# A fallback path written as a loop of 16 turns, its scratch laid out by block, and twelve first loads moved from ScalarE's DMA queue to SyncE's

## The chip, the cores and the metric

The kernel runs on one core of one Trainium2 chip. The metric is the device time of one execution in microseconds (us). Three runs of the kernel before gave 1262.43, 1261.22 and 1262.65 us, so the median is 1262.43 us.

## What is computed

One input `x` of 2048 rows and 512 columns goes through two branches, which are mixed row by row by a gate:

```python
def _A_ref(x, wq, wk, wv, wo):          # H = 32 query heads of 16, one shared key and value head
    q = (x @ wq).reshape(B, S, H, Dh).transpose(0, 2, 1, 3)
    k = x @ wk
    v = x @ wv
    scores = einsum("bhqd,bkd->bhqk", q, k) * (Dh ** -0.5)
    p = softmax(scores, axis=-1)
    o = einsum("bhqk,bkd->bhqd", p, v)
    return o.transpose(0, 2, 1, 3).reshape(B, S, H * Dh) @ wo
def _B_ref(x, w_gate, w_up, w_down):
    return (gelu(x @ w_gate) * (x @ w_up)) @ w_down
g = sigmoid((x * gate_w).sum(-1, keepdims=True))
out = g * a + (1 - g) * b
```

The weights `wq` and `wk` are drawn eight times larger than the others.

## The kernel before

**Prologue (the first 72 us).** `x` arrives transposed, in four groups of 512 rows. For each group TensorE projects K and V together (`pk`) and then four blocks of 128 columns of Q (`pq`, eight heads each). Every operand is split into a high part and a low part, and three products are summed. ScalarE and VectorE split each block of Q into `q2`, and `post_q` (L198) stores it to the scratch `scr` in DRAM with one DMA on SyncE's queue (SP), L213. The groups run in the order 1, 2, 3, 0, so that the last blocks stored are those of group 0, which attention reads first.

**Loads of Q.** Attention walks 64 half-blocks `u` of four heads (two buffers `Q`, one per `u` in turn). `load_q(u)` fills a buffer with six DMAs: four from `scr` (L275, L276) and two from the scratch `shs` (L285), which holds three extra rows per head that shift the exponent. In the general case these rows hold minus the row maximum; else they are zero, zero and one, written once by four DMAs on GpSimd's queue (L171). The loads of `u` = 0 and `u` = 1 are issued on ScalarE's queue (ACT), after the Q blocks 2 and 3 of the last group; all later ones on SP.

**The choice of path.** `pairmax` (L310) bounds the largest score from the largest absolute Q and K, sets `flag`, and fills one row, `zz[0:1]`, of 2048 values with a shift (L318), which two DMAs on ACT copy into rows 50 and 114 of the key tile `kp` (L320). All five engines then load `flag` into a register (L518) and branch (`tc.If`, L519). With these inputs the flag is 0 and the general path is skipped. The general path computes all scores once more to take the row maxima: written out, it is 2,048 matmuls, 1,024 reductions and 128 loads, and its code lies between the branch and what follows.

**DMA counters.** Each DMA on SP or ACT counts on one of eight semaphores (`DMAHW0` to `DMAHW7`), dealt in turn when the program is built. A DMA whose semaphore is still owed by an earlier one waits on its issuing engine until the earlier one has landed. On the path that is not taken, SP waits for all eight and then adds to each what the skipped path would have added (eight semaphore instructions at L519). What comes after the branch and reads loaded data waits for the counts after that addition.

**Main part.** 1024 score tiles: two matmuls (L576), one exponential on ScalarE (L579), four products with V (L649). Between them the matmuls of the second branch (L358) are dealt by the words of the table `WORDS`, two at a time on the two halves of the array. This order is fixed by hand and is the same before and after.

Of the kernel before, what the change touches and what calls it, by code (L numbers as in the profile page):

```python
# [9 lines left out]
F32 = mybir.dt.float32  # L10
# [9 lines left out]
P = 128  # L20
S = 2048
D = 512
H = 32
# [36 lines left out]
def mix_kernel(ctx, tc, xT, wq, wkv, wo, wf, out):  # L60
# [137 lines left out]
    def post_q(tg, b, pq, last):  # L198
        q2 = p2.tile([P, 2, TG], F32R, tag="q2", name=f"q2{tg}_{b}", bufs=3)
        i = tg * NB + b  # L200

        def bound():
            nc.vector.tensor_reduce(qmx[:, i : i + 1], pq, axis=AX, op=ALU.max, apply_absolute_value=True)
# [5 lines left out]
        nc.scalar.copy(q2[:, 0], pq)  # L209
        if not last:  # L210
            bound()
        nc.vector.tensor_sub(q2[:, 1], pq, q2[:, 0])
        nc.sync.dma_start(scr[tg, b].rearrange("(t d) h q -> (d h) t q", t=2), q2.bitcast(F32))  # L213

    chunks = [(tg, f) for tg in range(NTG) for f in range(NF)]
    W = {}
# [50 lines left out]

    Q = {}

    def load_qk(t, u, q):  # L270
        g, ub = divmod(u, 8)
        b, a = divmod(ub, 2)
        for j in range(2):
            hs = slice(4 * a + j, 4 * a + 4, 2)
            q.dma_start(t[64 * j : 64 * j + 32].bitcast(F32), scr[g, b, 0:32, hs])  # L275
            q.dma_start(t[64 * j + 32 : 64 * j + KR].bitcast(F32), scr[g, b, 0:16, hs])  # L276

    def load_q(u, shift=True, data=True, q=nc.sync):
        g, ub = divmod(u, 8)
        if data:  # L280
            Q[u] = cp.tile([P, 2, TG], F32R, tag="Q", name=f"Q{u}", bufs=2)
            load_qk(Q[u], u, q)
        if shift:
            for j in range(2):
                q.dma_start(Q[u][64 * j + KR : 64 * j + QK].bitcast(F32), shs[g, :, 4 * ub + j : 4 * ub + 4 : 2])  # L285

    fetch_w(0)
    fetch_w(1)
    for ti, tg in enumerate(order):
        xh, xl = xs[tg]  # L290
        pk = ps_a.tile([P, TG], F32, tag="pa", name=f"pk{tg}")
        passes(pk, lambda c: wkh[:, c], lambda c: wkl[:, c], lambda c: xh[:, c], lambda c: xl[:, c], NC)
        post_k(tg, pk)
        for b in range(NB):
            pq = two_banks(f"pq{tg}_{b}")[:, 0:TG]
            bs = slice(b * P, (b + 1) * P)
            passes(pq, lambda c: wqh[:, c, bs], lambda c: wql[:, c, bs], lambda c: xh[:, c], lambda c: xl[:, c], NC)
            if ti + 1 < NTG:
                split_x(order[ti + 1], b)
            post_q(tg, b, pq, ti == NTG - 1 and b == NB - 1)  # L300
            if ti == NTG - 1 and b == 0:
                for part in split_w(0):
                    part()
            if ti == NTG - 1 and b == 1:
                post_v()
            if ti == NTG - 1 and b >= 2:
                load_q(b - 2, q=nc.scalar)

    def pairmax():
# [6 lines left out]
        nc.vector.tensor_scalar(sh, cb, -1.01 * DH, None, op0=ALU.mult)  # L316
        row = zz[0:1].rearrange("p a b -> p (a b)")
        nc.vector.tensor_scalar(row, row, 0.0, sh[0:1], op0=ALU.mult, op1=ALU.add)  # L318
        for r in (QK - 1, 64 + QK - 1):
            nc.scalar.dma_start(kp[r : r + 1].bitcast(F32), row.bitcast(F32))  # L320

    acc = {}
    O = {}
# [195 lines left out]
    with tc.If(v > 0):  # L519
        with tc.tile_pool(name="gp", bufs=1) as gp:  # L520
            zr = gp.tile([1, S], F32, name="zr")
            nc.vector.memset(zr, 0.0)
            for r in (QK - 1, 64 + QK - 1):
                nc.sync.dma_start(kp[r : r + 1].bitcast(F32), zr)
            for g in range(NTG):
                mx = gp.tile([P, 4, H, 2], F32, tag="mx", name=f"mx{g}")
                for ub in range(8):
                    t = gp.tile([P, 2, TG], F32R, tag="gq", name=f"gq{g}_{ub}", bufs=2)
                    load_qk(t, 8 * g + ub, nc.sync)
                    for i in range(4):  # L530
                        for h in range(4):
                            rs = slice(64 * (h % 2), 64 * (h % 2) + KR)
                            for e in range(2):
                                ps = two_banks("gs")
                                for j in range(2):
                                    k0 = e * 1024 + j * 512
                                    nc.tensor.matmul(ps[:, j * 512 : (j + 1) * 512],
                                                     t[rs, h // 2, i * P : (i + 1) * P],
                                                     kp[rs, k0 : k0 + 512], start=True, stop=True)
                                nc.vector.tensor_reduce(mx[:, i, 4 * ub + h, e : e + 1], ps, axis=AX, op=ALU.max)  # L540
                m1 = gp.tile([P, 4, H], F32, tag="m1", name=f"m1{g}")
                nc.vector.tensor_reduce(m1, mx, axis=AX, op=ALU.max)
                pt = ps_f.tile([P, TG], F32, tag="pf", name=f"pt{g}")
                for i in range(4):
                    nc.tensor.transpose(pt[0:H, i * P : (i + 1) * P], m1[:, i], ident)
                nm = gp.tile([H, TG], F32, tag="nm", name=f"nm{g}")
                nb = gp.tile([H, 3, TG], F32R, tag="nb", name=f"nb{g}")
                nc.vector.tensor_scalar(nm, pt[0:H], -1.0, None, op0=ALU.mult)
                nc.vector.memset(nb[:, 2].bitcast(F32), 1.0)
                nc.vector.tensor_copy(nb[:, 0], nm)  # L550
                nc.vector.tensor_sub(nb[:, 1], nm, nb[:, 0])
                nc.sync.dma_start(shs[g].rearrange("r h q -> h r q"), nb.bitcast(F32))
# [217 lines left out]
```

## Time and profile before

| | |
|---|---|
| median of three runs | 1262.43 us (1261.22 to 1262.65) |
| span of the profiled execution | 1262.1 us |
| matmuls executed | 9,884 |
| TensorE / ScalarE / VectorE / GpSimd busy | 99% / 82% / 45% / 18% |
| instruction fetches, queues q8 and q14 | 80 packets and 35 packets |

No time of the profiled execution is listed beside its span of 1262.1 us; it lies 0.3 us under the median of the runs and inside their spread. In the views, PE is TensorE's matmuls and PEld its weight loads, DVE VectorE, ACT ScalarE, POOL GpSimd, SP SyncE; a name with a q behind it (SPq, PEq) is the engine's sequencer, that is an instruction that issues a DMA, branches, or handles a semaphore or register. Times in the views are counted from the first instruction.

### The profile page before, as it was taken

The numbers are of one execution on the slowest core, as the hardware profiler recorded it, in microseconds if no ns is written. First come the engines' busy times: TensorE is split into PE (matmuls) and PEld (weight loads), VectorE is DVE, ScalarE is ACT, GpSimd is POOL, SyncE is SP. The second block draws the span as 40 slices with busy tenths as digits, with TensorE's granted clock in tenths as the row PEclk, the third lists the DMA queues.
The fourth block names the chain that finished last, engine by engine and source line by source line (L and its number), as shares of the span: only waits on it lengthen the run. The fifth ranks groups of instructions, "written<-read, shape, count | busy, mean of one in ns | idle before, by whom it ended". The sixth has DMA issues, their size and how long they took to land.

```text
span 1262.1 us, 23901 instructions
## 1 busy us (share of the span) xinstructions
PE 1248.1 (99%) x9884; PEld 669.8 (53%) x9884; DVE 572.8 (45%) x860; ACT 1031.1 (82%) x1118; POOL 221.7 (18%) x261
## 2 busy tenths in 40 slices
PE   9989999999999999999999999999999999999998
PEld 6855555555455555545555555554544555455454
DVE  6762352635453163453546146362546324445334
ACT  5358888888898888888888888888887888888893
POOL 3132211201320020211131012120232002112100
PEclk9989999999999999999999999999999999999999
DMA  8441111111210111211030021011111013011000
GB/s 316 163 159 56 40 42 49 39 39 56 81 39 14 63 61 39 64 39 56 23 97 2 31 81 64 16 63 39 47 53 63 15 31 106 22 43 39 15 1 34
DMA packets 26371, 72.67 MB, mean 58 GB/s; under 512 B 4016, under 2 KB 4048, under 8 KB 26256
## 3 DMA queue, kind: packets, MB, share of 16 engines
q1 hardware_dynamic: 25244, 69.17, 16.5%
q8 instruction: 80, 1.31, 0.4%
q10 hardware_dynamic: 756, 1.11, 0.3%
q0 software_dynamic: 256, 0.79, 0.2%
q14 instruction: 35, 0.29, 0.1%
HBM read 57.67 MB, written 13.37 MB: 56 GB/s over the span
## 4 chain that ended last, share of the span: by engine, by line
PE 92%; ACT 1%; DVE 1%; issue 0%; POOL 0%; ACTq 0%
PE acc L649 37%; PE s L576 23%; PE z L358 18%; PE y L358 13%; ACT p L579 1%; PE wos L343 1%; DVE acc L466 0%; PE wof L343 0%; DVE sq L386 0%; POOL mark L366 0%; DVE sq L387 0%; DVE gs L394 0%; DVE n L600 0%; DVE gs L383 0%; ACT sq L390 0%
## 5 line engine op out<-in xcount | busy, mean ns | idle before, releaser
L579 ACT ACTIVATE p<-s 128x1024 f32<-128x1024 f32 x1024 | 979.8, 1025 | 176.2 <-PE s L576 169.0
L649 PE MATMUL acc<-p,v 128*32 128x512 f32 x4096 | 490.8, 598 | 0.0
L576 PE MATMUL s<-Q,kp 51*128 51x512 f32 x2048 | 392.2, 420 | 5.9 <-SPq L519 3.2
L576 PEld LDWEIGHTS s<-Q,kp 51*128 51x128 f32 x2048 | 188.1, 185 | 247.9 <-ACT p L579 167.5
L649 PEld LDWEIGHTS acc<-p,v 128*32 128x32 f32 x4096 | 107.7, 109 | 246.7 <-issue 241.1
L128 POOL TENSOR_TENSOR gl<-st,gh 128x512 fp32r<-128x512 f32 x88 | 123.9, 1429 | 400.1 <-PE s L576 177.4
L383 DVE COPY gs<-z 128x512 f32<-128x512 f32 x43 | 29.8, 692 | 247.6 <-PE z L358 124.6
L358 PE MATMUL y<-xh,gh 64*128 64x512 f32 x344 | 138.9, 404 | 1.5 <-DVE gs L394 1.5
L358 PE MATMUL z<-xh,gh 64*128 64x512 f32 x344 | 139.0, 404 | 0.7 <-POOL mark L366 0.7
L358 PE MATMUL z<-xl,gh 64*128 64x512 f32 x344 | 135.7, 394 | 0.0
L358 PE MATMUL y<-xl,gh 64*128 64x512 f32 x344 | 135.5, 394 | 0.0
L358 PE MATMUL y<-xh,gl 64*128 64x512 f32 x344 | 135.2, 393 | 0.0
L358 PE MATMUL z<-xh,gl 64*128 64x512 f32 x344 | 135.1, 393 | 0.0
L366 POOL MEMSET mark<- 1x1 f32 x81 | 8.5, 104 | 585.6 <-PE y L358 583.6
L456 DVE SCALAR_TENSOR_TENSOR acc<-z,gc,acc 128x512 f32<-128x512 f32 x24 | 18.0, 751 | 146.5 <-PE z L358 106.0
L358 PEld LDWEIGHTS z<-xh,gh 64*128 64x128 f32 x344 | 64.6, 188 | 16.0 <-POOL mark L366 8.8
L358 PEld LDWEIGHTS z<-xh,gl 64*128 64x128 f32 x344 | 64.3, 187 | 8.9
L358 PE MATMUL z<-dh,hh 64*128 64x512 f32 x176 | 69.0, 392 | 0.0
L358 PE MATMUL z<-dh,hl 64*128 64x512 f32 x176 | 68.9, 392 | 0.0
L358 PE MATMUL y<-dh,hh 64*128 64x512 f32 x176 | 68.9, 391 | 0.0
L358 PE MATMUL y<-dh,hl 64*128 64x512 f32 x176 | 68.8, 391 | 0.0
L358 PEld LDWEIGHTS z<-xl,gh 64*128 64x128 f32 x344 | 64.8, 188 | 7.6
(147 smaller groups left out, 1583.4 us busy)
## 6 DMA issues: line engine op xcount, KB each, us to landing
st<-wf SPq DMA_DIRECT2D x44, 768.0 KB
scr<-q SPq DMA_DIRECT2D x16, 512.0 KB
Q<-scr SPq DMA_DIRECT2D x60, 128.0 KB
out<-acc SPq DMA_DIRECT2D x16, 256.0 KB
Q<-scr SPq DMA_DIRECT2D x60, 64.0 KB
xr<-xT SPq DMA_DIRECT2D x6, 512.0 KB
xst<-xT SPq DMA_DIRECT2D x12, 256.0 KB
xr<-xT SPq DMA_DIRECT2D x4, 256.0 KB
```

The costliest lines, as they stand in the source:

```text
L128: eng_l.tensor_sub(lo, src, hi)
L343: nc.tensor.matmul(ps, a, b, start=(first and q == 0), stop=(last and q == len(terms) - 1), skip_group_check=True)
L358: mm = nc.tensor.matmul(ps, a[rs], b[rs], start=(half == 0 and q == 0), stop=(half == 1 and q == len(X) - 1), skip_group_check=True)
L366: relay = nc.gpsimd.memset(mark, 0.0).ins
L383: nc.vector.tensor_copy(gs, g)
L456: nc.vector.scalar_tensor_tensor(o, ps, w, o, op0=ALU.mult, op1=ALU.add)
L576: nc.tensor.matmul(ps[:, j * TG : (j + 1) * TG], kp[rs, kc * P : (kc + 1) * P], Q[u][rs, pr], start=True, stop=True)
L579: nc.scalar.activation(p, ps, AF.Exp, bias=0.0, scale=SCALE)
L649: nc.tensor.matmul(accp[u][32 * j : 32 * j + 32], vt[:, kc], pb[s, j // 2][:, (j % 2) * TG : (j % 2 + 1) * TG], start=(kc == 0), stop=(kc ...
```

## The change

Four edits go together. The general path becomes a loop over 16 blocks (`tc.For_i`), whose body handles two half-blocks. `scr` and `shs` are indexed by block, so that the loop can address them by a register; the initial fill of `shs` is four DMAs by head within a half-block in place of four by group of rows. The first twelve loads of Q go to SP's queue. The shift row has 512 values and is copied into `kp` four times over by a repeating source.

```diff
-    scr = dr.tile([NTG, NB, 32, 8, TG], F32, name="scr")
-    shs = dr.tile([NTG, 3, H, TG], F32, name="shs")
+    scr = dr.tile([NTG * NB, 32, 8, TG], F32, name="scr")
+    shs = dr.tile([NTG * NB, 2, 3, 4, TG], F32, name="shs")
...
-    for g in range(NTG):
-        nc.gpsimd.dma_start(shs[g].rearrange("r h q -> h r q"), zz[:, 0:3].bitcast(F32))
+    for h in range(4):
+        nc.gpsimd.dma_start(shs[:, :, :, h].rearrange("g a r q -> (g a) r q"), zz[:, 0:3].bitcast(F32))
...
-                load_q(b - 2, q=nc.scalar)
+                load_q(b - 2)
...
-        row = zz[0:1].rearrange("p a b -> p (a b)")
-        nc.vector.tensor_scalar(row, row, 0.0, sh[0:1], op0=ALU.mult, op1=ALU.add)
+        nc.vector.tensor_scalar(zz[0:1, 3], zz[0:1, 3], 0.0, sh[0:1], op0=ALU.mult, op1=ALU.add)
         for r in (QK - 1, 64 + QK - 1):
-            nc.scalar.dma_start(kp[r : r + 1].bitcast(F32), row.bitcast(F32))
+            nc.scalar.dma_start(kp[r : r + 1].bitcast(F32).rearrange("p (c q) -> p c q", c=4),
+                                zz[0:1, 3:4].bitcast(F32).broadcast_to([1, 4, TG]))
...
-            for g in range(NTG):
-                mx = gp.tile([P, 4, H, 2], F32, tag="mx", name=f"mx{g}")
-                for ub in range(8):
-                    t = gp.tile([P, 2, TG], F32R, tag="gq", name=f"gq{g}_{ub}", bufs=2)
-                    load_qk(t, 8 * g + ub, nc.sync)
+            with tc.For_i(0, NTG * NB, 1) as gb:
+                for a in range(2):
+                    t = gp.tile([P, 2, TG], F32R, tag="gq", name=f"gq{a}", bufs=2)
+                    load_qk(t, scr[bass.ds(gb, 1)].rearrange("o r h q -> (o r) h q"), a)
...
-            load_q(0, data=False)
-            load_q(1, data=False)
+            load_shift(0)
+            load_shift(1)
```

SP, from the store of the third Q block of group 0 to the branch (`scr<-q` is a store, `Q_587` and `Q_614` are the buffers of `u` = 0 and `u` = 1, and what a row waits for stands in brackets). Before:

```order
L213 DMA scr<-q_2_582 128x2x512 [waits DMAHW6_49,DVE_49,Activation_49]
L213 DMA scr<-q_3_607 128x2x512 [waits DMAHW5_49,DVE_49]
L518 TENSOR_LOAD flag [waits DVE_49]
L518 ISA x2
L519 COMPARE_AND_BRANCH
```

The same place on SP of the change, from the second load of `Q_587` to the last of `Q_614` (ahead of these rows stand the same store of the third block and the first load of `Q_587`, behind them the flag and the branch):

```order
L274 DMA Q_587<-scr 16x2x512 [waits DMAHW7_49]
L273 DMA Q_587<-scr 32x2x512 [waits DMAHW1_49]
L274 DMA Q_587<-scr 16x2x512 [waits DMAHW2_49]
L279 DMA Q_587<-shs 3x2x512 [waits DMAHW4_49,DMASW2_49,DMASW0_49]
L279 DMA Q_587<-shs 3x2x512 [waits DMAHW5_49,DMASW3_49,DMASW1_49]
L213 DMA scr<-q_3_607 128x2x512 [waits DMAHW6_49,DVE_49]
L273 DMA Q_614<-scr 32x2x512 [waits DMAHW7_49]
L274 DMA Q_614<-scr 16x2x512 [waits DMAHW0_49]
L273 DMA Q_614<-scr 32x2x512 [waits DMAHW1_49]
L274 DMA Q_614<-scr 16x2x512 [waits DMAHW2_49]
L279 DMA Q_614<-shs 3x2x512 [waits DMAHW3_49]
L279 DMA Q_614<-shs 3x2x512 [waits DMAHW4_49]
```

Twelve loads now stand ahead of SP's load of the flag, and the store of the last block stands behind six of them. The store of the third block now counts on semaphore 5 and the first load of `Q_587` on 6, so the last load of `Q_587` waits until that store has landed, and the store of the last block waits until that first load has. The semaphores 0 and 3, which the loads of `Q_587` skip in the turn, are those of the two copies into `kp` on ACT: the second load of `Q_614` waits for the first copy to land, and the fifth for the second copy.

ACT, from its last conversion of Q to the copies into `kp`. Before:

```order
L209 CAST q_3_607<-pq_3_594 128x512 [waits DVE_49,Activation_49]
L275 DMA Q_614<-scr 32x2x512 [waits DMAHW4_49]
L276 DMA Q_614<-scr 16x2x512 [waits DMAHW6_49]
L275 DMA Q_614<-scr 32x2x512 [waits DMAHW7_49]
L276 DMA Q_614<-scr 16x2x512 [waits DMAHW0_49]
L285 DMA Q_614<-shs 3x2x512 [waits DMAHW1_49]
L285 DMA Q_614<-shs 3x2x512 [waits DMAHW2_49]
L320 DMA kp<-woh 1x16x128 [waits DMAHW3_49,DVE_49]
L320 DMA kp<-woh 1x16x128 [waits DMAHW4_49]
```

And in the change:

```order
L209 CAST q_2_582<-pq_2_569 128x512 [waits DVE_49,DMAHW2_49,PE_49,Activation_49]
L209 CAST q_3_607<-pq_3_594 128x512 [waits DMAHW3_49,DVE_49,Activation_49]
L318 DMA kp<-woh 1x4x512 [waits DVE_49]
L318 DMA kp<-woh 1x4x512
L517 TENSOR_LOAD flag [waits DVE_49]
L518 COMPARE_AND_BRANCH
```

ACT's two copies into `kp` follow its last conversion directly and wait for VectorE alone.

TensorE, the whole of what lies between its branch and the first score matmul in the change (`gs` are the scores of the general path, `pt` its transposed maxima):

```order
L518 COMPARE_AND_BRANCH
L524 COMPARE_AND_BRANCH
L524 UNCONDITIONAL_BRANCH x2
L764 BRANCH_PREFETCH_HINT
L536 MATMUL gs<-kp,gq_708 128x512 x64
L544 MATMUL pt_844<-ident,m_842 4x128 x4
L536 MATMUL gs<-kp,gq_856 128x512 x64
L544 MATMUL pt_992<-ident,m_990 4x128 x4
L524 REGISTER_ALU
L524 COMPARE_AND_BRANCH
L524 UNCONDITIONAL_BRANCH
L518 UNCONDITIONAL_BRANCH x2
```

Before, 32 rows of 64 such matmuls and four of four transposes stood there: 2,064 matmuls, each with a weight load, against 136 now. On VectorE 1,024 reductions became 64, and on SP 128 loads became eight. Behind the branch the order on every engine is that of before.

More of the change, by code (lines that the diff above doesn't have):

```diff
@@ L212, in post_q @@
         nc.vector.tensor_sub(q2[:, 1], pq, q2[:, 0])
[L213 removed]
+        nc.sync.dma_start(scr[i].rearrange("(t d) h q -> (d h) t q", t=2), q2.bitcast(F32))
     chunks = [(tg, f) for tg in range(NTG) for f in range(NF)]
@@ L268, in mix_kernel, with load_qk, load_shift, load_q @@
     Q = {}
-    def load_qk(t, u, q):
-        g, ub = divmod(u, 8)
-        b, a = divmod(ub, 2)
+    def load_qk(t, rows, a):
         for j in range(2):
             hs = slice(4 * a + j, 4 * a + 4, 2)
[L275 to L285, printed above, removed]
+            nc.sync.dma_start(t[64 * j : 64 * j + 32].bitcast(F32), rows[0:32, hs])
+            nc.sync.dma_start(t[64 * j + 32 : 64 * j + KR].bitcast(F32), rows[0:16, hs])
+    def load_shift(u):
+        gb, a = divmod(u, 2)
+        for j in range(2):
+            nc.sync.dma_start(Q[u][64 * j + KR : 64 * j + QK].bitcast(F32), shs[gb, a, :, j::2])
+    def load_q(u):
+        Q[u] = cp.tile([P, 2, TG], F32R, tag="Q", name=f"Q{u}", bufs=2)
+        load_qk(Q[u], scr[u // 2], u % 2)
+        load_shift(u)
     fetch_w(0)
```

27 lines of the change are left out of this document (14 added, 13 removed).

## The prediction

> **What bounds the kernel now.** I read the page first, then the waits, then one place closely.
>
> ```profile
> span 1262.1 us, 23901 instructions
> PE 1248.1 (99%) x9884; PEld 669.8 (53%) x9884; DVE 572.8 (45%) x860; ACT 1031.1 (82%) x1118; POOL 221.7 (18%) x261
> PE 92%; ACT 1%; DVE 1%; issue 0%; POOL 0%; ACTq 0%
> q8 instruction: 80, 1.31, 0.4%
> ```
>
> TensorE is busy 99% of the span and holds 92% of the chain that ended last. So a microsecond that TensorE loses or wins anywhere moves the end by about as much. The change leaves TensorE's order alone, so I look for what TensorE waits for where the change acts, around the branch at 60 to 80 us. The waits name it:
>
> ```profile
> PEld s L576 <- PEq L519: 3.5, 1, 3.5
> PE s L576 <- SPq L519: 3.2, 1, 3.2
> DVE dh L127 <- DVEq L519: 1.9, 1, 1.9
> PE s L576 <- issue: 1.4, 1, 1.4
> ```
>
> ```profile
> 72.65 0.70 PE L576 MATMUL s<-Q,kp 51*128 51x512 f32 x2 [3.15 <-SPq L519]
> ```
>
> Before the first score matmul, at 72.65 (start, duration, and in brackets the idle time before it), TensorE's matmuls stand still for 3.15 us, that is from 69.5, released by SP's semaphores of the branch; shortly after they do so for another 1.4 us for which no waiting shows. A third loss is only seen in the clock. These are stretches of 3.41 us; the columns are the stretch, its length, then the busy time of PE, PEld, DVE, ACT and POOL (instructions), the granted clock, DMA share and GB/s.
>
> ```profile
> 63.66:67.07 3.41, 3.41 (x18) 2.72 (x16) 2.41 (x9) 0.59 (x1) 0.00 (x0) 1.00 1.00 319
> 67.07:70.49 3.42, 2.42 (x11) 1.69 (x9) 2.52 (x4) 0.00 (x0) 1.16 (x1) 1.00 0.70 224
> 70.49:73.90 3.41, 1.25 (x8) 1.07 (x9) 2.41 (x3) 0.46 (x1) 3.05 (x3) 1.00 0.26 41
> 73.90:77.31 3.41, 2.02 (x11) 1.82 (x10) 2.54 (x5) 2.18 (x3) 0.07 (x1) 0.50 0.86 252
> 77.31:80.73 3.42, 3.42 (x19) 3.37 (x16) 0.58 (x1) 1.63 (x3) 0.00 (x0) 0.50 0.46 188
> 80.73:84.14 3.41, 3.41 (x30) 2.63 (x28) 2.46 (x5) 3.26 (x5) 2.11 (x3) 1.00 0.00 0
> 954.54:957.95 3.41, 1.94 (x15) 1.28 (x17) 3.26 (x6) 1.79 (x3) 0.00 (x0) 1.00 0.00 0
> 957.95:961.36 3.41, 3.41 (x20) 2.66 (x18) 3.41 (x4) 1.77 (x3) 3.03 (x2) 0.50 0.00 0
> ```
>
> After a stretch in which PE was busy 1.25, 2.02 or 1.94 us the next one ran at half clock; after 2.42 us or more it ran at full clock. So the stall costs more than its length: 73.90 to 80.73 us holds 2.02 + 3.42 us of work at half speed, 2.72 us lost. TensorE loses here 3.2 + 1.4 + 2.7 = 7.3 us in all, and that is what the change can move.
>
> **The branch itself.** Columns of the next view: line, engine, operation, count, duration min/median/max in ns, first and last start in us.
>
> ```profile
> L519 SPq EVENT_SEMAPHORE  x8: 17/17/17, 71.7 to 72.5; - x8
> L519 DVEq COMPARE_BRANCH  x1: 72/72/72, 68.1 to 68.1; - x1
> L519 PEldq COMPARE_BRANCH  x1: 3892/3892/3892, 68.1 to 68.1; - x1
> L519 SPq COMPARE_BRANCH  x1: 45/45/45, 68.4 to 68.4; - x1
> L519 DVEq EVENT_SEMAPHORE  x1: 21/21/21, 71.3 to 71.3; - x1
> L519 ACTq COMPARE_BRANCH  x1: 54/54/54, 71.9 to 71.9; - x1
> ```
>
> TensorE's branch takes 3.9 us, to 72.0; VectorE's next instruction comes 3.2 us behind its branch; on ACT, where nothing is skipped, a branch takes 0.05 us. Packets of the instruction queues lie in the same stretch (69 to 71.4 us, first fence), and one more on q8 at 72.7 to 74.4 us, the place of the second stall (second fence):
>
> ```profile
> q8 instruction: 1, 0.02, 3.0%
> q14 instruction: 2, 0.02, 2.9%
> ```
>
> ```profile
> q8 instruction: 1, 0.02, 5.3%
> ```
>
> So I read the branch as a jump to code that is not there yet. On the page q8 brought 1.31 MB in 80 packets for 2 x 9,884 TensorE instructions, some 250 a packet. The jump was over 2,064 matmuls with weight loads, about 4,130 instructions or 16 packets; it becomes 136, about 270. I take it that the target is then there and that both q8 stalls go: **minus 1.4 us** for the second; the first only uncovers the other wait. The Trainium skill, page "Runtime: NRT & Kernel Launch", section "Instruction fetch mechanics", says that instructions are fetched in blocks of 256, the next block while one runs, and that a taken branch out of these two blocks waits for a fetch. The packets agree; by that rule 270 instructions are within reach only from the first part of a block, and about a hundred, as on SP and VectorE, from any. Out of reach, the 1.4 us could come back, and the sum below would be plus 0.4.
>
> **The other wait: SP's eight semaphores.** They end at 72.5, TensorE starts at 72.65. Before, what lands last ahead of them are the copies into `kp`, late because ACT issues the loads of `u` = 1 first:
>
> ```profile
> 64.64 0.59 ACT L209 CAST q<-pq 128x512 fp32r<-128x512 f32 x1 [2.95 <-DVE qmx L203]
> 64.66 0.31 ACTq L275 DMA_DIRECT2D Q<-scr  x1
> 67.13 0.31 ACTq L276 DMA_DIRECT2D Q<-scr  x1
> 69.21 1.81 ACTq L320 DMA_DIRECT2D kp<-woh  x2
> ```
>
> ```profile
> 63.07 3.27 SPq L213 DMA_DIRECT2D scr<-q  x2
> ```
>
> ```profile
> 66.82 0.13 DVE L316 TENSOR_SCALAR sh<-cb 1x1 f32<-1x1 f32 x1
> 67.05 1.27 DVE L318 TENSOR_SCALAR woh<-woh,sh 1x2048 fp32r<-1x2048 f32 x1
> ```
>
> The load at 67.13 stood until the store issued at 63.07 had landed, 4.06 us; the copies were issued by 71.02 and had landed within 1.5 us of that, by SP's last semaphore. In the change ACT is free. The row has 512 values: 0.13 + (1.27 - 0.13) / 4 = 0.42 us, so it is ready at 67.4, and the first copy goes out 1.8 us sooner than before. It lands between 69.0 (1.5 us later, the issue free) and 71.5 (4.06 later); I take 69.8, by the row of the copies themselves: 0.9 us of issue, half of 1.81, and 1.5.
>
> But SP now issues the loads, and the second load of `u` = 1 waits for that first copy. Behind it stand four more loads, SP's load of the flag, and the eight semaphores, for which TensorE waits. SP's price for loads and flag:
>
> ```profile
> 112.48 0.42 SPq L276 DMA_DIRECT2D Q<-scr  x1
> 114.54 0.36 SPq L227 DMA_DIRECT2D st<-wf  x1
> ```
>
> ```profile
> L518 SPq TENSOR_LOAD <-flag x1: 1060/1060/1060, 66.9 to 66.9; - x1
> ```
>
> The last five of six such loads take 114.54 - 112.48 = 2.06 us: done at 71.9. The flag's load started at 66.9 and the branch came at 68.4: 1.5 us, to 73.4. Eight semaphores, 71.7 to 72.5, are 0.8 us: 74.2. The last load, issued at about 71.6, lands by 73.4 at best and 75.7 at worst. The rest of the SP chain lies ahead of it: the store issued at 63.07 lands by 67.1, then the last store and the first load of `u` = 1 go out by 68, before the copy has landed; that costs nothing unless the copy lands before 68. So TensorE resumes at **74.2** instead of 72.65 (73.4 with the copy at 69.0, 77.6 in the first rival): plus 1.55 us. Behind SP's loads and flag stands the first weight fetch of the main part:
>
> ```profile
> 72.65 1.95 SPq L227 DMA_DIRECT2D st<-wf  x2
> ```
>
> ```profile
> 81.62 0.76 DVE L127 CAST gh<-st 128x512 fp32r<-128x512 f32 x2
> ```
>
> It has 9 us until VectorE splits its weights at 81.6, of which 1.55 go; no term, and if the cover were short, at most that much.
>
> **The clock after it.** With the stretches where they are, 70.49 to 73.90 is idle and 73.90 to 77.31 runs at half clock, with 3.1 us of work: full clock from 77.31, loss 1.55 us against 2.72, so **minus 1.2 us**. If the stretches fall elsewhere the loss is 1.1 to 2.8 us.
>
> **The rest at nothing.** The first six loads that leave ACT stood in the 2.95 us in which its conversion waited for VectorE, so that stays at 64.64. VectorE's 1.9 us and 0.85 us of the shorter row come free while TensorE stands still, so they are hidden; without that cover they would be worth 2.7 us at most. The fill of `shs` is four DMAs of 192 KB before and after, issued 50 us ahead of their readers.
>
> **Sum.** Before 3.15 + 1.4 + 2.7 = 7.25; after 4.7 (69.5 to 74.2) + 0 + 1.55 = 6.25. That is minus 1.0 us on a span of 1262.1; on the median of 1262.43, which is 0.3 above the span, **1261.4 us**. About 0.2%, or 2.5 us, is what a measurement of this kernel can tell from no change.
>
> **Rivals.**
> *The SP chain runs late (slower).* If each landing takes the 4.06 us of the store, the copy lands at 71.5, the loads end at 73.5, the last lands at 77.3 and TensorE resumes at 77.6: 8.1 idle and 1.6 of clock, 9.7 against 7.25, 1264.9 us. It decides at about 75.2: later than that, the stretch to 77.31 holds under 2.1 us of work and the half clock lasts to 80.73. For it: the stores and loads did take that long at 60 to 67 us. Against it: that was with the DMA engines 100% and 70% busy up to 70.49, and 26% after it. Chance 0.2.
> *The short code does not shorten the jump.* TensorE's 3.9 us stay hidden (72.0 is before 74.2), but SP's own branch comes at 73.4 and 3.3 us (68.4 to 71.7 before) go on top: resumed at 77.5, again 2.3 us worse, 1264.7. For it: no row shows a jump over a hundred instructions. Against it: ACT's 0.05 us. Chance 0.12.
> *SP's loads wait for nothing that matters.* Twelve loads at 0.41 from 63.45 end at 68.4; the last lands at 71.0, between 1.5 and 4.06 us behind, and the semaphores end at 71.2. TensorE is idle for 1.8 us, the stretch from 70.49 holds 2.6 us of work, and by the 2.42 row the clock stays: 1.8 against 7.25, so 1257.0. Chance 0.08, since the order shows the waits. The Trainium skill, page "DMA: Bandwidth & Descriptors", section "Issuing engines are not separate DMA queues", says that the issuing engine only decides who spends the issue time; by that alone this case would hold. In this trace the wait at 67.13 speaks against it.
>
> **How the numbers follow.** The forecast has 0.6: 1261.4, and 1259.6 to 1262.8 by itself, the stretches' 1.1 to 2.8 and the half-clock stretch at 957.95, which costs 1.7 us and may or may not return when everything shifts by 1 us. The range, 1258.8 to 1265.2, takes in both slower rivals' prices and leaves out the third rival. Faster than 1259.9: 0.08 from the third rival and 0.09 from the forecast, 0.17. Slower than 1264.95: half of 0.32, with a little less as both lie just under it, 0.14. Within: 0.69.
>
> **What would show it.** TensorE's branch under 0.2 us and no q8 packet right behind it; VectorE's wait at the branch gone. SP's first load of `u` = 1 by 68, the second near 69.8, its flag at 71.9, its semaphores ending near 74.2, and TensorE idle 69.5 to 74.2 with no second stall; half clock for one stretch. Copies into `kp` out at 67.4. Wrong would be: SP's semaphores 3 us behind its branch, a resumption before 73 or after 75.2, or a difference that arises behind 85 us.

## The result and the profile after

| | before | change |
|---|---|---|
| median | 1262.04 us (1261.13 to 1263.56, 6 runs) | 1266.22 us (1265.68 to 1266.86, 6 runs) |
| ratio | | 1.0034, 95% interval 1.0022 to 1.0045 |
| span of the profiled execution | 1262.1 us | 1265.1 us (its time: 1266.86 us) |

The change is 4.2 us slower; 1261.4 us was predicted. The page of the change first, as far as it answers to that of before:

```profile
span 1265.1 us, 23904 instructions
PE 1246.6 (99%) x9884; PEld 668.5 (53%) x9884; DVE 573.2 (45%) x860; ACT 1030.4 (81%) x1118; POOL 222.4 (18%) x261
q8 instruction: 79, 1.29, 0.4%
```

TensorE has the same work (1248.1 us before), so the loss is waiting. The waits show one of 7.6 us where before had 3.2 and 1.4, and the instructions of the branch show which engine came last:

```profile
PE s L574 <- SPq L518: 7.6, 1, 7.6
```

```profile
L518 SPq EVENT_SEMAPHORE  x8: 17/17/17, 76.2 to 76.7; - x8
L518 PEldq COMPARE_BRANCH  x1: 352/352/352, 67.4 to 67.4; - x1
L518 DVEq COMPARE_BRANCH  x1: 72/72/72, 67.7 to 67.7; - x1
...
L518 SPq COMPARE_BRANCH  x1: 45/45/45, 75.6 to 75.6; - x1
```

TensorE's branch takes 0.35 us instead of 3.9, and SP's semaphores follow its branch by 0.6 us instead of 3.3: the short code does what it was expected to do. (Not all of the 3.3 us is the jump: a load of `u` = 1 landed at 71.68 in before, just ahead of the first semaphore. Experiments 3 and 15 have 2.5 and 2.7 us with nothing left to land.) But SP branches at 75.6 instead of 68.4. The timeline of the change shows why (start, duration; SP's rows, and between them the copies on ACT and TensorE's first score matmul):

```profile
65.74 1.77 SPq L279 DMA_DIRECT2D Q<-shs  x2
67.42 1.80 ACTq L318 DMA_DIRECT2D kp<-woh  x2
67.62 0.42 SPq L213 DMA_DIRECT2D scr<-q  x1
68.09 0.45 SPq L273 DMA_DIRECT2D Q<-scr  x1
71.64 0.31 SPq L274 DMA_DIRECT2D Q<-scr  x1
71.99 0.42 SPq L273 DMA_DIRECT2D Q<-scr  x1
72.46 0.42 SPq L274 DMA_DIRECT2D Q<-scr  x1
72.93 1.48 SPq L279 DMA_DIRECT2D Q<-shs  x2
76.83 0.84 SPq L227 DMA_DIRECT2D st<-wf  x2
76.93 0.89 PE L574 MATMUL s<-Q,kp 51*128 51x512 f32 x2 [7.58 <-SPq L518]
```

The second load of `u` = 1 stood from 68.5 to 71.64, until the first copy into `kp`, issued at 67.42, had landed: 4.2 us. SP's own waits name it (us in total, times, longest):

```profile
SPq L274 <- DMA kp<-woh: 3.1, 1, 3.1
```

Behind it stand four loads (the two of shift rows take 1.48 us), the flag, the branch at 75.6 and the eight semaphores. The clock then pays as well (columns as in the prediction):

```profile
67.07:70.49 3.42, 2.29 (x11) 1.55 (x9) 3.27 (x6) 0.00 (x0) 2.09 (x2) 1.00 0.60 192
70.49:73.90 3.41, 0.00 (x0) 0.00 (x0) 2.90 (x2) 0.00 (x0) 2.38 (x2) 0.64 0.34 101
73.90:77.31 3.41, 0.38 (x2) 0.41 (x3) 0.00 (x0) 0.00 (x0) 0.00 (x0) 0.50 0.03 10
77.31:80.73 3.42, 3.42 (x18) 3.42 (x19) 1.14 (x2) 2.56 (x3) 0.00 (x0) 0.50 0.79 296
80.73:84.14 3.41, 3.41 (x25) 2.82 (x24) 1.61 (x5) 2.47 (x4) 0.09 (x1) 0.86 0.41 169
```

The trace puts the half clock from 71.45 to 81.69 us (0.64 and 0.86 are means of stretches that hold both clocks). From 76.93 on that is 4.76 us of work at half speed, 2.4 us lost. The loss at the branch is 7.58 + 2.4 = 9.96 us, against 7.25 before: 2.7 us more. The spans differ by 3.0 us.

### The profile page after: what moved, and what is told of

It is laid out like the page before. It is cut to its first block, busy times and chain, and to the rows that moved or that the text cites. A ratio compares the mean times of both kernels' runs of the same rounds, so it can differ in the third digit from the quotient of the medians.

```text
span 1265.1 us, 23904 instructions
## 1 busy us (share of the span) xinstructions
PE 1246.6 (99%) x9884; PEld 668.5 (53%) x9884; DVE 573.2 (45%) x860; ACT 1030.4 (81%) x1118; POOL 222.4 (18%) x261
## 4 chain that ended last, share of the span: by engine, by line
PE 91%; DVE 1%; ACT 1%; POOL 0%; issue 0%; ACTq 0%
PE acc L647 37%; PE s L574 22%; PE z L357 18%; PE y L357 13%; ACT p L577 1%; PE wos L342 1%; POOL gl L128 0%; DVE acc L465 0%; PE wof L342 0%; DVE ol L623 0%; POOL mark L365 0%; DVE sq L385 0%; DVE oh L619 0%; DVE acc L455 0%; DVE xh L127 0%
## 5 line engine op out<-in xcount | busy, mean ns | idle before, releaser
L357 PE MATMUL z<-dl,hh 64*128 64x512 f32 x176 | 68.7, 390 | 0.0
```

The lines of the kernel that those rows point to most:

```text
L357: mm = nc.tensor.matmul(ps, a[rs], b[rs], start=(half == 0 and q == 0), stop=(half == 1 and q == len(X) - 1), skip_group_check=True)
```

## Experiments

All times are medians; "idle" is TensorE's wait ahead of its first score matmul in the profile, 3.15 us before and 7.58 in the change; "resumed" is when that matmul starts. The ratio is to runs of before that were made along with the experiment; the medians of these batches differ by up to 0.8 us. The diffs are cut to the lines that make the edit.

| edit | us | ratio to before, 95% interval | idle | resumed |
|---|---|---|---|---|
| 1 before, unchanged | 1261.85 | 1.0001 (0.9992 to 1.0010) | 3.13 | 71.61 |
| 2 change, twelve loads on ACT | 1262.29 | 0.9999 (0.9990 to 1.0008) | 4.13 | 74.15 |
| 3 before, twelve loads on SP | 1266.60 | 1.0037 (1.0023 to 1.0051) | 8.63 | 78.56 |
| 4 change, second Q behind the branch | 1264.02 | 1.0015 (1.0006 to 1.0024) | 3.69 | 72.35 |
| 5 change, no store beside the copies | 1264.96 | 1.0025 (1.0015 to 1.0034) | 6.22 | 75.00 |
| 6 change, both Q in one piece | 1265.82 | 1.0032 (1.0019 to 1.0046) | 6.67 | 75.63 |
| 7 change, five rows of heads in `shs` | 1264.88 | 1.0022 (1.0012 to 1.0032) | 5.96 | 74.65 |
| 8 change, 16 SP loads more | 1267.34 | 1.0044 (1.0030 to 1.0058) | 7.73 | 76.60 |
| 9 change, Q split on SP and ACT | 1263.59 | 1.0011 (1.0002 to 1.0020) | 5.29 | 74.47 |
| 10 = 2 with five rows | 1260.74 | 0.9989 (0.9980 to 0.9998) | 3.23 | 71.92 |
| 11 change, one VectorE instruction more | 1265.94 | 1.0029 (1.0017 to 1.0041) | 7.47 | 76.31 |
| 12 = 10, second Q in attention | 1258.79 | 0.9980 (0.9971 to 0.9989) | 1.46 | 70.28 |
| 13 change, unchanged | 1266.28 | 1.0037 (1.0023 to 1.0051) | 7.63 | 76.71 |
| 14 = 11, beside 13 | 1266.25 | 1.0037 (1.0023 to 1.0051) | 7.63 | 76.65 |
| 15 before, second Q in attention | 1261.27 | 1.0001 (0.9992 to 1.0010) | 2.82 | 71.47 |

**1. Before, unchanged.** 

> The kernel before, unchanged, as a control. Both theories: 1262 us, ratio 1.000. It is there to see which of the places at which the traces of before and of the change differ also differ between two executions of one kernel: the half-clock stretch at 958 us (1.7 us), the landing of the last output (2.3 us behind the last VectorE instruction in before, 3.5 in the change) and the time outside the span. Theory A (the whole loss is at the branch) expects that these wander by a microsecond or more here as well. Theory B (the change also costs something behind the branch) expects them as they were in before: stretch there, 2.3 us.

Its profile has what before's has, as theory B expected: 3.13 and 1.43 us of stalls, a half-clock stretch near 957 us, and the same end (4.0 us from the last matmul to the end of the span, 5.2 in the change). Its eleven executions spread from 1261.00 to 1263.97 us, each about 1.75 us above its span, so single traces compare to about a microsecond, and the medians decide.

**2. The twelve loads back on ACT.** 

> The change with its twelve first loads of Q back on ACT's queue; loop, short row and scratch by block stay. Theory A (SP's serial chain of waits is the loss, the short code itself is good): SP goes from the last store straight to the flag, as in before; TensorE's branch is short and the 1.4 us stall at 75.5 is gone; TensorE resumes near 72, and the time is 1259 to 1261 us, 5 to 7 under the change. Theory B (loop, layout or row cost by themselves): the time stays above before, 1264 to 1266 us, although SP issues no load. Theory C (the fetch of code was hidden anyway, and only the queue matters): as before, 1262, resumed at 72.5.

```diff
-                load_q(b - 2)
+                load_q(b - 2, q=nc.scalar)
```

The loss is gone, so it came with the loads. But nothing is won either. The first view has the loads of shift rows on ACT (duration min/median/max in ns), the second is the timeline:

```profile
L279 ACTq DMA_DIRECT2D Q<-shs x4: 717/736/1356, 63.8 to 70.0; - x4
```

```profile
70.83 1.34 ACTq L318 DMA_DIRECT2D kp<-woh  x2
74.15 1.05 PE L574 MATMUL s<-Q,kp 51*128 51x512 f32 x2 [4.13 <-SPq L518]
```

The copies go out 1.6 us later than before (69.21), although the row is ready sooner: a load of shift rows costs 0.74 us here, 0.30 before. TensorE waits 1 us longer, saves the second stall and has half clock for 3.41 us instead of 6.83, so that by the 1,000th matmul this trace has won 1.0 us on before's since the 100th; by the 7,400th, near 950 us, it has lost that again, and no run here shows why. Theory A had the queue right and the gain wrong.

**3. Only the loads moved, in before.** 

> The kernel before with one edit, its twelve first loads of Q on SP's queue; unrolled path, long row and old scratch stay. Theory A: the loads of the second Q stand behind the landings of the copies into kp as in the change, and the long row makes these 0.8 us later; SP's own jump then adds its 3.3 us behind the flag, TensorE resumes near 80 and the time is 1266 to 1270 us, above the change. Theory B (the loop or the layout is the loss): near before, 1262 to 1263 us.

```diff
-                load_q(b - 2, q=nc.scalar)
+                load_q(b - 2)
```

This one edit costs as much as the whole change. In the timeline of SP, here the third load of `u` = 1 waits for the first copy, from 69.1 to 72.73:

```profile
68.39 0.72 SPq L276 DMA_DIRECT2D Q<-scr  x1
72.73 0.30 SPq L275 DMA_DIRECT2D Q<-scr  x1
```

The copy, issued at 68.78, took 3.9 us, to 72.71. The last store, sent at 67.36, had landed at 70.64; two loads of `u` = 1, sent between the two, landed at 72.40 and 72.56. Behind SP's branch at 75.3 come 2.5 us of its jump, which the change does not have, so TensorE is idle 8.63 us. So the moved loads alone bring the loss, which is theory A (it put the time above the change; it is level). The loop is not the loss; what the layout of the scratch adds, experiment 7 shows.

**4. The second Q behind the branch.** 

> The change with the six loads of the second Q issued behind the branch instead of ahead of it, still on SP's queue. Theory A: SP has only the six loads of the first Q ahead of the flag, none of which waits for a copy into kp; the flag is loaded at about 68.3, SP's branch is at 69.8, and only its semaphores still wait for the copies' landing at 71.6 to 72.5, so that TensorE resumes at 72.5 to 73, 3 to 4 us idle instead of 7.6; 1259 to 1262 us. Theory B: the loss stays, 1265 to 1266 us.

```diff
-            if ti == NTG - 1 and b >= 2:
-                load_q(b - 2)
+            if ti == NTG - 1 and b == 2:
+                load_q(0)
...
-            load_shift(1)
+    load_q(1)
```

TensorE is back 4.6 us sooner than in the change, as theory A said, but the time falls by 2.2 us only and stays some 2 us above before. The timeline shows where the rest goes (SP, VectorE, ACT and TensorE in turn):

```profile
75.76 0.89 SPq L227 DMA_DIRECT2D st<-wf  x2
...
79.99 0.77 DVE L127 CAST gh<-st 128x512 fp32r<-128x512 f32 x2 [0.87 <-DMA st<-wf]
...
85.61 0.63 ACT L389 ACTIVATE sq<-sq 128x512 f32<-128x512 f32 x1 [2.13 <-DVE sq L386]
...
88.11 0.73 PE L574 MATMUL s<-Q,kp 51*128 51x512 f32 x4 [1.31 <-ACT p L577]
...
89.45 3.60 PE L647 MATMUL acc<-p,v 128*32 128x512 f32 x16
```

The six loads now stand ahead of the weight fetch. It goes out at 75.76, 3.4 us behind TensorE's start; in before (72.65) and in the change the two come together. VectorE waits for it, ACT for VectorE, TensorE for ACT's exponentials (1.31 us, before 0.27), and 16 products take 3.60 us at half clock (before 1.92). The prediction had named that fetch as work behind SP's loads, with 9 us of cover; the cover is used up here.

**5. No store beside the copies.** 

> The change, with the store of the last Q block left out and the store of the block ahead of it made twice instead, some 4 us earlier (the output is then not the reference's: heads of the last block read the block ahead). As many bytes, as many loads on SP, the same waits; only, no store goes out beside the two copies into kp. Theory A (the copies land late because their packets stand behind the 512 KB of the last store): the first copy lands some 2.5 us after its issue starts instead of 4.2, at about 70, SP's loads end at about 73, TensorE resumes near 75 instead of 76.9, and the time is 1.5 to 3 us under the change. Theory B (the copies take 4 us by themselves, by their shape or ACT's queue): 4 us again, 76.9, no gain beyond 0.5 us.

```diff
-        nc.sync.dma_start(scr[i].rearrange("(t d) h q -> (d h) t q", t=2), q2.bitcast(F32))
+        for k in ((i, i + 1) if (tg, b) == (0, NB - 2) else () if last else (i,)):
+            nc.sync.dma_start(scr[k].rearrange("(t d) h q -> (d h) t q", t=2), q2.bitcast(F32))
```

Timeline of the copies, of the load that waits for the first of them, and of TensorE:

```profile
66.85 2.00 ACTq L319 DMA_DIRECT2D kp<-woh  x2
68.34 0.40 SPq L274 DMA_DIRECT2D Q<-scr  x1
69.72 0.32 SPq L275 DMA_DIRECT2D Q<-scr  x1
75.00 0.99 PE L575 MATMUL s<-Q,kp 51*128 51x512 f32 x2 [6.22 <-SPq L519]
```

The copy lands 2.85 us after its issue starts instead of 4.2, and TensorE resumes 1.9 us sooner, both near theory A's numbers; the time falls by 1.3 us, a little less than its 1.5 to 3. The other way round, experiment 4 has the store beside the copies and no load behind it, and its copy took 4.2 us. Most other runs sort the same way. With the store sent 0.2 us behind the first copy, the copy took 4.1 to 4.3 us in 8, 11, 13 and 14; with the store 0.6 us ahead of it, 3.7 in 7; with no store under way, 2.6 in before and 2.8 in 2 and in 6. But a store under way is not enough: in 9 and 12 it was sent 1.3 and 1.6 us ahead of the copy and had not landed, and the copy took 2.1 us. In 3, where it was sent 1.4 us ahead, the two loads behind it landed with the copy.

**6. Both Q in one piece.** 

> The change with all twelve loads in one piece: the second Q is loaded right behind the first one, ahead of the last store, so that none of its loads stands in the turn behind a copy into kp. This is the third rival of the prediction made on purpose. Theory A (the wait of SP's loads for the copies is the loss): no stop of 3.5 us between the first and second load of the second Q; the twelve loads end near 70 at 0.4 to 0.7 us each, the last store goes out there, and its landing 3 to 5 us later sets the semaphores: TensorE resumes at 73 to 75, 2 to 4 us earlier than in the change. Theory B (SP's time for twelve loads and not the wait): resumed at 76 or later, as in the change.

```diff
-            if ti == NTG - 1 and b >= 2:
-                load_q(b - 2)
+            if ti == NTG - 1 and b == 2:
+                load_q(0)
+                load_q(1)
```

My premise failed: the turn of the counters gave the third load of the second Q the counter of the first copy, and it waited from 68.0 to 69.86. The last store then went out at 72.36, and its landing 2.8 us later set the end. A gain of 0.4 us in the medians does not tell the two theories apart; it does show that moving a DMA in the order only moves the wait.

**7. Five rows of heads.** 

> The change with one size altered: the scratch of shift rows has five rows of heads instead of four, of which four are used. In the traces a load of shift rows costs its queue 0.28 us with the scratch of before and 0.72 us with that of the change, 64 times of 64. Theory A (with four rows the two strides of the source fall into one even step, and that is what makes it slow): 0.28 us again, the last two loads of the second Q end 0.9 us earlier, TensorE resumes near 76.0 and the time falls by about 0.9 us. Theory B (the order of the scratch, block by block, costs it): 0.72 us again and the time of the change.

```diff
-    shs = dr.tile([NTG * NB, 2, 3, 4, TG], F32, name="shs")
+    shs = dr.tile([NTG * NB, 2, 3, 5, TG], F32, name="shs")
```

The loads of shift rows, in the change and with five rows:

```profile
L279 SPq DMA_DIRECT2D Q<-shs x64: 706/723/927, 65.7 to 1176.7; - x64
```

```profile
L279 SPq DMA_DIRECT2D Q<-shs x64: 242/288/337, 65.1 to 1173.3; - x64
```

The slices that read and write `shs` follow. Theory A: 0.29 us again, and 1.3 us of the loss gone (0.9 expected); the copy also landed sooner here (3.7 us instead of 4.2), since with faster loads the store went out 0.6 us ahead of it instead of 0.2 behind. So the order by block is not what costs, but something that goes with four rows; that the two strides fall into one step is an inference and was not looked at further.

**8 and 11. The packet at the end.** First sixteen loads on SP more, then one VectorE instruction more, both ahead of a score tile of `u` = 20:

```diff
+        if pr == 0 and kc == 8 and u == 20:
+            for k in range(16):
+                nc.sync.dma_start(tiny[0:1, k : k + 1], xT[0][0:1, 0, k : k + 1])
```

```diff
+        if pr == 0 and kc == 8 and u == 20:
+            nc.vector.memset(tiny[0:1, 0:1], 0.0)
```

> The change with sixteen loads of four bytes more on SP's queue in the middle of the program, where SP is idle: they do nothing but put SP's last instructions further on in its code. In the change one packet of 8 KB on an instruction queue lies within the last output's transfer, and the last semaphore comes 2.8 us behind the last store's start instead of 1.7; in the kernel before no such packet lies there. Theory A (the fetch of SP's next block of code delays the end): the packet moves away from the end, the last landing comes 1.1 us earlier, and the time is 1 to 1.2 us under the change. Theory B (the end is late for another reason): no difference.

> The change with one VectorE instruction more, a memset of one value in the middle of the program. The packet of code that lies within the last output's transfer was not SP's, since sixteen more instructions on SP left it in its place. Of the kernels without it, the one with its first loads on ACT differs from the change in ACT's code by fifteen instructions, in VectorE's by one. Theory A (it is VectorE's code): the packet leaves the end, the last landing comes 1.1 us earlier, and the time is 1 us under the change. Theory B (it is ACT's): it stays, and so does the time.

The DMA view of the last 3 us of the change has a packet of code that before's has not, and SP's semaphores end later. Here the queue's row (packets, MB, share), then the last semaphores in the change and with one VectorE instruction more (first and last start):

```profile
q14 instruction: 1, 0.01, 0.6%
```

```profile
L764 SPq EVENT_SEMAPHORE  x12: 17/28/28, 1261.1 to 1265.0; - x12
```

```profile
L767 SPq EVENT_SEMAPHORE  x12: 17/28/28, 1261.4 to 1264.3; - x12
```

Sixteen instructions more on SP left the packet in its place; one more on VectorE (a memset in the middle of attention) moved it from 1262.5 to 1250.5 us, and the end came 1.1 us sooner behind the last matmul (which ends at 1259.87 and 1260.19). So it is VectorE's code. All traces of the short code agree: the packet lies at the end where VectorE has 990 instructions, branches and semaphores included, and the span then ends 5.2 us behind the last matmul; with 991 it lies 9.5 us or more ahead of that matmul's end, and the span ends 4.2 us behind it. But the median fell by 0.3 us only, and the sixteen loads cost 1.1 us.

**13 and 14. The change and experiment 11 beside each other, unaltered.** 

> The change once more, unaltered, as the control for the next run on the same chip: 1266 us, the packet of code within the last output's transfer, the last landing 3.1 us behind the last store's start.

> The change with one VectorE instruction more, once more beside the change itself. In the profile of its first run the packet had left the end and the last landing came 1.06 us earlier, but its median stood only 0.3 us under that of the change, which ran at another time. Theory A (the packet at the end is a part of the loss): 0.8 to 1.1 us under the change on the same chip. Theory B (what the end wins is lost elsewhere, or lies within the spread): under 0.4 us.

Theory B: 1266.28 and 1266.25 us. The end without the packet does not show in the medians. In the trace of 14 the matmuls stand 0.7 us later than in 13 by the 6000th, and another 1.7 us behind a half-clock stretch at 960 us; whether that belongs to the edit or to the execution, these runs don't tell.

**9. Q split over both queues.** 

> A version put together from what the runs before it showed: loop and short row as in the change, the scratch of shift rows with five rows of heads (0.28 us a load), the first Q loaded on SP and the second on ACT, both behind the third block, so that no load stands behind a copy into kp or ahead of the flag. Theory A (SP's chain was the whole loss): SP loads the flag near 67, its branch is at 68, and its semaphores end when the copies and the last store have landed, at 70.5 to 72; TensorE resumes there, idle 1.5 to 2.5 us instead of 7.6, and has no stall behind it: 1258 to 1260 us. Theory B (what TensorE wins at the branch is given back at about 88 us, where it waits for ACT's exponentials, as in the run with the second Q loaded late): resumed as early, but level with before from 95 us on, 1261 to 1263 us.

```diff
-            if ti == NTG - 1 and b >= 2:
-                load_q(b - 2)
+            if ti == NTG - 1 and b == 2:
+                load_q(0)
+                load_q(1, q=nc.scalar)
```

It has the five rows of 7 as well. Neither theory: TensorE resumes at 74.47. ACT's timeline:

```profile
66.56 0.32 ACTq L274 DMA_DIRECT2D Q<-scr  x1
...
67.95 0.59 ACT L209 CAST q<-pq 128x512 fp32r<-128x512 f32 x1 [6.57 <-DMA Q<-shs]
70.61 1.32 ACTq L319 DMA_DIRECT2D kp<-woh  x2
```

The fourth load on ACT had the counter of a store on SP and stood from 62.4 to 66.56, and with it ACT's conversion (64.64 before), the flag and the copies. A counter shared by two queues lets a DMA of one stop the engine of the other.

**10. Loads on ACT, five rows.** 

> The change with its twelve first loads back on ACT's queue and the scratch of shift rows with five rows of heads. Theory A: the four loads of shift rows on ACT cost 0.3 us each instead of 0.7 to 1.4, so the copies into kp go out some 2 us sooner than in the same kernel with four rows (70.83), land near 71.5, and TensorE resumes near 72 instead of 74.1: 1260 to 1261 us, a little under before, since TensorE's code fetch behind the branch is gone as well. Theory B (given back at 88 us): 1262 us, as with four rows.

The edits are those of 2 and 7 together.

Copies and TensorE in the timeline, then the stretches ahead of the half clock, which here starts at 73.60:

```profile
68.24 1.62 ACTq L318 DMA_DIRECT2D kp<-woh  x2
71.92 0.77 PE L574 MATMUL s<-Q,kp 51*128 51x512 f32 x2 [3.23 <-SPq L518]
```

```profile
66.78:70.19 3.41, 1.90 (x9) 1.25 (x7) 3.27 (x5) 0.00 (x0) 2.46 (x2) 1.00 0.55 176
70.19:73.60 3.41, 1.68 (x13) 1.59 (x14) 2.52 (x2) 0.82 (x1) 2.01 (x2) 1.00 0.26 31
```

Theory A: the copies go out at 68.24 and TensorE resumes at 71.92. It is 1.05 us faster than before, the first version whose interval lies under 1.

**12. The second Q in attention.** 

> Put together from the runs: loop and short row as in the change, five rows of heads in the scratch of shift rows, the first Q loaded on ACT ahead of its conversion as in before, the second Q not ahead of the branch at all but on SP in the third step of attention, like all later ones. Ahead of the branch ACT then has nothing between its conversion and the copies into kp, and SP nothing but stores and the flag. Theory A (the last landing ahead of the branch sets TensorE's start, and the loads of the second Q were what made it late): copies out at about 66.5, landed by 69 to 70.5; TensorE resumes at 70 to 71, idle 1 to 2 us, no half clock or one stretch: 1258 to 1260 us. Theory B (the gain at the branch is given back at 85 to 90 us, where TensorE waits for ACT): 1261 to 1262 us although it resumes there.

On top of 10:

```diff
-            if ti == NTG - 1 and b >= 2:
-                load_q(b - 2, q=nc.scalar)
+            if ti == NTG - 1 and b == 2:
+                load_q(0, q=nc.scalar)
...
-        if pr == 0 and kc == 2 and u >= 1 and u + 1 < 8 * NTG:
+        if pr == 0 and kc == 2 and u + 1 < 8 * NTG:
```

The general path no longer loads shift rows for the second Q. TensorE's row in the timeline, and the stretches around it (those of before's trace; in this one a boundary lies at 70.14, and the stretch from 66.73 to it has 2.09 us of TensorE's work):

```profile
70.28 0.70 PE L573 MATMUL s<-Q,kp 51*128 51x512 f32 x2 [1.46 <-SPq L518]
```

```profile
67.07:70.49 3.42, 1.96 (x9) 1.32 (x8) 3.27 (x5) 0.00 (x0) 2.62 (x2) 1.00 0.20 71
70.49:73.90 3.41, 3.29 (x26) 2.86 (x25) 2.68 (x3) 1.97 (x3) 1.88 (x2) 1.00 0.82 238
73.90:77.31 3.41, 2.76 (x20) 1.77 (x22) 3.04 (x8) 3.41 (x6) 0.14 (x2) 1.00 0.94 283
```

Theory A: 1.46 us idle and full clock throughout. At 1258.79 us it beats both kernels, by 2.9 and 7.5 us.

**15. The same move without the short code.** 

> The kernel before with the second Q loaded in the third step of attention instead of ahead of the branch, and nothing of the change: unrolled general path, long row, old scratch, first Q on ACT. It tells what the short code is worth once no load stands in the way (with the short code the same edit gave 1258.8). Theory A (the short code pays as soon as the landings come early): SP's branch is at about 67.5, its semaphores start 3.3 us behind it when its code has come, at 71, as TensorE's own code does at 72; TensorE resumes at 71.5 to 72, and has the stall of 1.4 us behind it: 1260 to 1261.5 us, some 2 us above the same edit with short code. Theory B (the jump was hidden all along and only the loads matter): resumed near 70, 1258.5 to 1259.5 us.

The edit is that of 12, made in the kernel before; the general path, which is skipped, no longer loads shift rows for the second Q.

The branch in this kernel, then TensorE's rows:

```profile
L519 SPq EVENT_SEMAPHORE  x8: 17/17/17, 70.2 to 71.3; - x8
...
L519 PEldq COMPARE_BRANCH  x1: 3672/3672/3672, 67.3 to 67.3; - x1
```

```profile
71.47 0.70 PE L575 MATMUL s<-Q,kp 51*128 51x512 f32 x2 [2.82 <-DVE dh L127]
...
74.63 0.79 PE L575 MATMUL s<-Q,kp 51*128 51x512 f32 x1 [1.63 <-issue]
```

Theory A: 1261.27 us, level with before. With the long code SP's semaphores start 2.7 us behind its branch (67.5), TensorE's branch takes 3.7 us, to 71.0, and the second stall of 1.6 us is back. The long row holds TensorE as well: the second copy lands at 71.23, against 70.05 in 12. These ends and that of VectorE's split of the weights (`dh`, the last, which the row names) lie within 0.4 us of one another, so these runs don't tell what the code and the row are worth singly. Short code, short row and the scratch that goes with them are worth 2.5 us here (1261.27 to 1258.79). With the loads of the second Q still ahead of the branch they were worth 1.05 us in 10, and with slow loads of shift rows nothing in 2.

## Why the prediction was wrong

- **The copy into `kp`: the step that failed.** "I take 69.8, by the row of the copies themselves": it landed at 71.62. That row was taken where the last store had been sent 3.2 us earlier (65.98, copies at 69.21) and had landed. The freed ACT sends the copies at 67.42, as I had said, and SP sends the store at 67.62, beside them. I had both times, 67.4 and "by 68", and put their meeting at nothing. The upper bound, 71.5, was the store's 4.06 us; it was the value to take, and experiments 4 and 5 show the store to be the reason in this order. This is 1.8 us of the 2.7 by which TensorE resumed later (76.93 against 74.2).
- **Five loads behind it, 2.06 us.** 2.77 us, since the loads of shift rows cost 0.72 us in the new scratch. This is 0.7 us. I had counted that scratch at nothing and looked only at its fill. Experiment 7, with 0.29 us a load, has 1.91 us here (70.50 to 72.41).
- **Flag and branch 1.5, semaphores 0.8.** 1.2 and 1.1 us (74.41 to 75.64 and to 76.7), together as predicted. In sum 74.2 became 76.7, TensorE follows 0.2 us later, and the idle time is 7.58 instead of 4.7 us.
- **The clock, 1.55 us after.** 2.4 us: TensorE resumed past 75.2, the point from which the first rival was to decide, and the half clock lasted to 81.69. My reading of the rows of before (up to 2.02 us of work in a stretch, then half clock) is no fixed rule: in experiment 10 a stretch with 1.90 us was followed by full clock.
- **The first rival was the case as far as the copy goes.** Its copy lands at 71.5 (71.62). But it also had the last load land 4.06 us after its issue and TensorE wait for that. The last load landed at 76.12, 2.4 us after its issue, before SP came to its semaphores at 76.17: SP's loads, flag and branch set the end. That its 77.6 and 9.7 us stand close to 76.93 and 9.96 is in part luck: 0.5 us too much idle time against 0.8 too little half clock. Its 1264.9 is 1.3 us under the median. I had argued against it with DMA engines that were 26% busy after 70.49; the trace of before could say that only of its own order of transfers.
- **The short code.** Right: a branch of 0.35 us (I had asked for under 0.2), no second stall. The jump over 136 matmuls brought no wait, that over 2,064 one of 3.7 us (experiment 15). The Trainium skill ("Runtime: NRT & Kernel Launch", section "Instruction fetch mechanics") with its blocks of 256 fits this. I had worked that rule out too narrowly: by it, as an estimate, a jump over 270 instructions stays within two blocks from 242 of the 256 places of the first (512 less 270), which is nearly all of it. But the 1.4 us were no gain where a longer wait stood ahead of them.
- **The third rival**, which the same skill's page "DMA: Bandwidth & Descriptors" (section "Issuing engines are not separate DMA queues") would give, does not hold here: moving twelve loads to another issuing engine, and nothing else, cost 4.8 us (experiment 3). What a rule on issue time leaves out is the time that the issuing engine stands still: 3.1 us at one load of the change.
- **The base.** I set the span of 1262.1 beside the median of 1262.43. Every run lies about 1.75 us above its span, so that execution took some 1263.9 us, at the upper end of all of before's runs, with a half-clock stretch of 1.7 us at 958 us that the profiled execution of the change lacks. Seven of experiment 1's eleven executions were granted 0.997 of the full clock and took 1261.35 us in the median, the other four 0.996 and 1263.38, so most seem to go without that stretch; none of before without it was profiled.
- **The rest of the difference.** The spans differ by 3.0 us. By the times of the same matmuls in the two traces, the change falls 2.7 us behind from the 100th (where it is 0.1 ahead) to the 1,000th, another 0.7 up to the 7,400th, wins 1.5 at the stretch at 958 us, and loses 1.2 behind the last matmul. The 0.7 has no cause shown; the two traces of before differ by 0.3 there. My own sign of being wrong, a difference that arises behind 85 us, is thus met too: I had no term for the end. In the medians, which differ by 4.2 us, the branch is shown; the end, which the traces show, did not show in 13 and 14. How the rest divides stays open.

## What to carry to other kernels

Before you move a DMA to an idle queue, list what stands behind it on that queue and on which semaphore it will count: a DMA that waits for an earlier one's landing stops its engine, and with it the flag, the branch and the next fetch. Price a landing by a row with the same traffic beside it; an earlier issue may only meet another transfer. And shorten a jump only together with the wait that covers it: the short code brought nothing in experiment 2, 1.05 us in 10, and 2.5 us once the second Q's loads were out of the way.

## What the runs showed of the hardware

- A small copy (8 KB) landed 4.1 to 4.3 us after its issue began where a store of 512 KB was sent 0.2 us behind it (the change, 4, 8, 11, 13, 14), 3.7 where it was sent 0.6 us ahead (7), 2.6 to 2.9 with none under way (before, 2, 5, 6, 10), and 2.1 with one sent 1.3 or 1.6 us ahead and not yet landed (9, 12). It took 3.9 in 3, where two loads were sent between store and copy, and 3.1 in 15, with the store 2.4 us ahead.
- The same load of six rows of 2 KB cost its queue 0.28 us or 0.72 us, depending on how many rows of heads the DRAM tensor has that it reads: 0.28 with 32 or five, 0.72 with four.
- A packet of VectorE's code fell into the last output's transfer in the profiles of the change and of experiments 4 to 8 and 13, and the span ended 5.2 us behind the last matmul there; in those that had one VectorE instruction more (2, 9 to 12 and 14) it did not, and the span ended 4.2 us behind it.
